# Other steps for the scores and transposes of three batches, for the sums of w2 and for the stores of two experts' w2

## The chip, the core and the metric

The kernel runs on one core of a Trainium2 chip. Its engines each run their own list of instructions in program order: PE (TensorE, the matmuls), DVE (VectorE), ACT (ScalarE), POOL (GpSimd) and SP (SyncE, which here only issues transfers). POOL and ACT issue transfers too. Between engines, work is ordered by semaphores. The metric is the time of one execution on the device in microseconds (us), as the median of the runs.

## The reference

The program is an attention over 32 memory slots followed by a mixture of four experts. All inputs are fp32.

```python
# q, k, v: (8, 8, 576, 64); phi: (8, 8, 576, 32)
a = softmax(phi, axis=seq)
k_m = einsum('bhsm,bhsd->bhmd', a, k)
v_m = einsum('bhsm,bhsd->bhmd', a, v)
attn = softmax(q @ k_m.T / sqrt(64), axis=-1) @ v_m
x = attn.transpose(0, 2, 1, 3).reshape(8 * 576, 512)
# experts: w1 (4, 512, 1024), w2 (4, 1024, 512), p = probs / sum(probs)
out = sum(p[:, e] * (relu(x @ w1[e]) @ w2[e]) for e in range(4))
```

## The kernel before

Every fp32 operand of a large product is kept as two parts, a rounded high part and the rest, and a product is three matmuls of the parts (high by high, high by rest, rest by high), added up in a PSUM bank. A split is a copy on ACT (the high part) and a subtraction on DVE or POOL (the rest).

The attention of a batch is never written out. `attn @ w1[e]` is computed as the softmax weights `AT` (32 slots of 8 heads by 576 rows) times `vw`, which is `v_m` times `w1[e]`. For experts 0 to 2 of the first four batches `vw` is made in place (L535 to L537). For expert 3 of these, and for the last four batches later on, one matmul pair makes it for four batches at once, the "four-batch products": L159 and L160 split the weight, L579 multiplies, L584 and L585 write the two parts into one of three buffers `vst`, POOL stores the buffer to memory (L567, `vwd`), and SP loads the pieces back as `vw` (L618).

**Steps.** The first four batches are worked off in two pairs of 128 steps each: 4 experts by 2 batches by 2 row halves by 8 column tiles of the hidden layer. Step s first adds up what the last group of eight has finished (`accumulate`, L696 on DVE), then runs what a table `plan` holds for s, then makes the hidden tile of step s + 2 (`first`: six matmuls L641 to L643, 256 or 320 wide, then the relu on ACT, L653, and its rest on DVE, L655) and the second product of step s (`second`: L674 to L676, 512 wide, six or nine matmuls). So a relu has two steps before its tile is used. From step 256 on come 64 units of four steps each, which do the last two pairs of batches with seven products of half-sized blocks instead of eight; these need sums of blocks of w2.

**What fills the plan.** `at(s, ...)` puts work into step s; nothing else decides the order.

- `attention(b, start, written, scores, turns)` does one batch's attention. Its numbers stand in the table `ATT`. phi is loaded at `start`, and k and v are multiplied from there on; `written` is where `v_m` is split. `scores` holds three steps n, for query tiles 0 and 1, 2 and 3, and 4: the score matmuls L463 at n, the maximum on DVE (L473, L476) at n + 1, the exponential on ACT (L483) at n + 2, the rest of the softmax on DVE (L490 to L493) at n + 3. `turns` holds three steps n: the transposes on PE (L514, which read L493's result `at`) at n, and the copies into `AT` (L525 on ACT, L526 on DVE) at n + 1, which give the bank back.
- `sums(s, home, lag, e, fh)` makes the sums for one half of an expert's w2; the table `JOBS` holds s, home and lag of each of the eight jobs, numbered from 0. At s SP loads two halves of a megabyte into the buffer `raw` (L201); there is one such buffer, so the load waits on SP until the last store of the job before has landed. At s + lag and s + lag + 1 DVE makes four sums (L225 to L228); at s + lag + 1 to s + lag + 4 ACT (L213) and POOL (L214) split them; at s + lag + 3 and s + lag + 5 POOL stores them (L219). In jobs of home "" the split parts live in buffers that a batch's phi and tail also use.
- `keep_w2(e, j)` stores the split w2 of the first pair in memory (L182, eight transfers of 0.5 MB per expert, by POOL for experts 1 to 3), to be loaded later. They are issued at steps 32 e + `KEEP_AT` + j.
- SP's loads of inputs go through four buffers `stage` (L145); taking one issues the load three further on in the order of use. The query tiles of the scores come this way, as `in_qm` and, for the last tile, `in_qt`.

Of the kernel before, what the change touches and what calls it, by code (L numbers as in the profile page):

```python
# [27 lines left out]
STEPS = 2 * 2 * NJ  # L28
PAIR = E * STEPS
# [21 lines left out]
PAIR_AT = ((18, 19, 26, 27), (28, 29, 30, 31))  # L51

ATT = {
    2: (22, 48, (92, 96, 100), (97, 101, 104)),
    3: (38, 65, (104, 107, 110), (112, 113, 114)),
    4: (PAIR, PAIR + 35, (PAIR + 34, PAIR + 37, PAIR + 41), (PAIR + 38, PAIR + 42, PAIR + 45)),
    5: (PAIR + 26, PAIR + 53, (PAIR + 76, PAIR + 80, PAIR + 84), (PAIR + 112, PAIR + 113, PAIR + 114)),
    6: (PAIR + 40, PAIR + 67, (2 * PAIR + 23, 2 * PAIR + 27, 2 * PAIR + 31), (2 * PAIR + 29, 2 * PAIR + 33, 2 * PAIR + 37)),
    7: (PAIR + 64, PAIR + 90, (2 * PAIR + 98, 2 * PAIR + 102, 2 * PAIR + 106), (2 * PAIR + 115, 2 * PAIR + 116, 2 * PAIR + 117)),
}  # L60

# [9 lines left out]
Q = 256  # L71
X_BANK, Y_BANK, AB_BANK = 4, 2, 6
JOBS = (
    (62, "", 4), (86, "", 4), (97, "", 4), (108, "", 4), (118, "", 4),
    (PAIR + 26, "AT", 4), (PAIR + 61, "a", 3), (PAIR + 87, "", 4),
)
KEEP_AT, W2_AGAIN = 20, 24
FOUR_AT_7 = ((0, 4, 8, 12), (16, 20, 24, 28))
VW_LOAD_7 = ((21, 37), (26, 41))
FIRST_LOADS = (PAIR + 112, PAIR + 121, PAIR + 122, PAIR + 123, PAIR + 124, PAIR + 125, PAIR + 126, PAIR + 127)  # L80
# [3 lines left out]
def body(ctx: ExitStack, tc: tile.TileContext, qm, qt, kv, kvt, phi, prob, w1, w1d, w2, out):  # L84
# [95 lines left out]
    def keep_w2(e, j):  # L180
        d = kept_for["w2", e, j] = dram.tile([P, 2, DM], F32, name=f"kw{e}{j}")
        (nc.gpsimd if e else nc.scalar).dma_start(d, w2t[0, e, j].bitcast(F32))  # L182
# [521 lines left out]
    def at(s, unit):  # L704
        plan[s].append(unit if isinstance(unit, tuple) else (None, unit))
# [112 lines left out]
        attention(b, *ATT[b])  # L818
    for e in range(E):
        for j in range(NJ):  # L820
            at(e * STEPS + KEEP_AT + j, lambda a=(e, j): keep_w2(*a))
    for n, job in enumerate(JOBS):
        sums(*job, n // 2, n % 2)
    for s in FIRST_LOADS:
# [19 lines left out]
    for block in range(UNITS // 4):  # L844
        e, fh = divmod(block % (2 * E), 2)
# [428 lines left out]
```

## Time and profile before

| | |
|---|---|
| median of 3 runs | 1399.04 us (1397.17 to 1401.68) |
| profiled execution | 1398.29 us, its span 1396.2 us |
| PE busy | 1365.6 us (98%) |
| DVE, ACT, POOL busy | 838.1, 625.5, 617.2 us (60%, 45%, 44%) |
| mean DMA traffic | 216 GB/s over the span |

A row of the timeline gives the start and the duration of an instruction in us, its engine, its line, what it writes and reads, and in brackets how long the engine stood before it and who ended that. Matmuls overlap: the time that one takes from PE is the distance from its start to the next one's, not its printed duration. `SPq` is the queue of transfers that SP issues. A row of the windows gives, for a stretch of time, the busy time of each engine with its number of instructions, then the granted TensorE clock as a share of the full one, the busy share of the DMA engines and what they moved.

### The profile page before, as it was taken

To read this page: it belongs to the slowest core of one execution; us is meant where nothing else is said; L and a number is where in the kernel's file an instruction comes from. 1 tells how busy PE (TensorE), PEld (TensorE's weight loads), DVE (VectorE), ACT (ScalarE), POOL (GpSimd) and SP (SyncE) were. 2 spreads that over 40 slices of the span, in tenths; PEclk is the share of its full clock that TensorE was granted. 3 is DMA by queue.
4 is the path that set the end of the run, shared out by engine and by line. 5 is a ranking of instruction groups with operands and counts; after the bars stand their busy time and mean duration, and the time that the engine had idled before them with its cause. 6 is when DMAs were issued, how large, how long until landed. Compare 5 with 4: busy or idle time off the path is not lost.

```text
span 1396.2 us, 25220 instructions
## 1 busy us (share of the span) xinstructions
PE 1365.6 (98%) x8894; PEld 1250.9 (90%) x8894; DVE 838.1 (60%) x1894; ACT 625.5 (45%) x1536; POOL 617.2 (44%) x652
## 2 busy tenths in 40 slices
PE   7999999999999999999999999999999999999998
PEld 6788888887878888889888998999999999999998
DVE  7875535446645365454434477767767666666666
ACT  6665555534335455554334344455443333333332
POOL 4400355755343415533145376677753344433333
PEclk9999999999999999999999999999999999999999
DMA  7742336798575354354599898999984776666662
GB/s 254 240 163 76 123 102 223 250 362 288 200 292 207 100 198 164 122 197 135 174 295 304 265 326 283 309 329 316 329 290 143 241 196 176 176 176 176 175 179 79
DMA packets 102029, 301.37 MB, mean 216 GB/s; under 512 B 24976, under 2 KB 26128, under 8 KB 101904
## 3 DMA queue, kind: packets, MB, share of 16 engines
q1 hardware_dynamic: 81168, 224.26, 51.8%
q0 software_dynamic: 19584, 71.31, 13.1%
q10 hardware_dynamic: 1152, 4.19, 0.8%
q8 instruction: 71, 1.16, 0.3%
q14 instruction: 54, 0.44, 0.1%
HBM read 213.46 MB, written 84.93 MB: 214 GB/s over the span
## 4 chain that ended last, share of the span: by engine, by line
PE 73%; DVE 3%; DMA 3%; POOL 2%; issue 1%; ACT 1%; SPq 0%; DVEq 0%; POOLq 0%; ACTq 0%
PE banks L1002 22%; PE banks L674 6%; PE banks L675 6%; PE banks L676 6%; PE banks L916 5%; PE banks L917 5%; PE banks L918 5%; PE banks L641 3%; PE banks L642 3%; PE banks L643 3%; PE banks L579 2%; PE banks L463 2%; PE banks L357 1%; PE banks L1040 1%; PE banks L1041 1%
## 5 line engine op out<-in xcount | busy, mean ns | idle before, releaser
L1020 DVE SCALAR_TENSOR_TENSOR acc<-banks,pt,acc 128x256 f32<-128x256 f32 x416 | 200.0, 481 | 108.9 <-PE banks L1002 105.2
L160 POOL TENSOR_TENSOR w<-stage,w 128x512 fp32r<-128x512 f32 x134 | 176.6, 1319 | 191.2 <-ACT w L159 180.9
L655 DVE SCALAR_TENSOR_TENSOR h<-banks,h 128x256 fp32r<-128x256 f32 x256 | 107.5, 421 | 174.1 <-ACT h L653 106.6
L674 PE MATMUL banks<-w,h 128*128 128x512 f32 x512 | 203.0, 396 | 1.4 <-DVE acc L696 1.3
L676 PE MATMUL banks<-w,h 128*128 128x512 f32 x512 | 201.9, 394 | 1.9 <-DVE h L655 1.9
L675 PE MATMUL banks<-w,h 128*128 128x512 f32 x512 | 202.3, 395 | 0.0
L653 ACT ACTIVATE h<-banks 128x256 fp32r<-128x256 f32 x256 | 97.9, 384 | 206.8 <-PE banks L643 163.8
L641 PE MATMUL banks<-AT,vw 128*128 128x256 f32 (+1 forms) x512 | 156.7, 306 | 3.9 <-DVE vw L556 2.1
L1002 PE MATMUL banks<-w,a 128*128 128x256 f32 x1080 | 154.7, 282 | 0.3 <-DVE acc L1020 0.2
L643 PE MATMUL banks<-AT,vw 128*128 128x256 f32 (+1 forms) x512 | 151.0, 296 | 1.2 <-DVE vw L556 1.2
L916 PE MATMUL banks<-AT,vw 128*128 128x256 f32 (+1 forms) x512 | 151.8, 296 | 0.0
L642 PE MATMUL banks<-AT,vw 128*128 128x256 f32 (+1 forms) x512 | 151.5, 296 | 0.2 <-DVE AT L526 0.2
L917 PE MATMUL banks<-AT,vw 128*128 128x256 f32 (+1 forms) x512 | 151.3, 295 | 0.0
L918 PE MATMUL banks<-AT,vw 128*128 128x256 f32 (+1 forms) x512 | 151.0, 295 | 0.0
L1002 PEld LDWEIGHTS banks<-w,a 128*128 128x128 f32 x1080 | 143.6, 189 | 4.8 <-issue 0.9
L983 POOL TENSOR_TENSOR vt<-ph,vt 128x512 fp32r<-128x512 f32 x64 | 84.1, 1314 | 107.8 <-ACT vt L982 78.2
L346 POOL TENSOR_TENSOR kvs<-stage,kvs 128x512 fp32r<-128x512 f32 x58 | 75.2, 1316 | 104.8 <-ACT kvs L345 98.7
L676 PEld LDWEIGHTS banks<-w,h 128*128 128x128 f32 x512 | 96.8, 189 | 24.0 <-DVE h L655 2.3
L641 PEld LDWEIGHTS banks<-AT,vw 128*128 128x128 f32 x512 | 96.7, 189 | 14.6 <-DVE vw L556 4.8
L674 PEld LDWEIGHTS banks<-w,h 128*128 128x128 f32 x512 | 96.8, 189 | 13.7 <-DVE acc L696 1.7
L675 PEld LDWEIGHTS banks<-w,h 128*128 128x128 f32 x512 | 96.9, 189 | 10.9
L159 ACT CAST w<-stage 128x512 fp32r<-128x512 f32 x168 | 102.8, 619 | 4.6 <-DMA stage<-in_w 2.3
(149 smaller groups left out, 2982.5 us busy)
## 6 DMA issues: line engine op xcount, KB each, us to landing
w<-kw SPq DMA_DIRECT2D x93, 512.0 KB, 5.5
vwd<-vst POOLq DMA_DIRECT2D x80, 512.0 KB, 6.2
vw<-vwd SPq DMA_DIRECT2D x320, 128.0 KB, 5.7
w<-v SPq DMA_DIRECT2D x55, 512.0 KB, 5.7
stage<-in_w SPq DMA_DIRECT2D x44, 512.0 KB, 4.4
stage<-in_w1d SPq DMA_DIRECT2D x40, 512.0 KB, 4.9
stage<-in_kv SPq DMA_DIRECT2D x32, 512.0 KB, 4.1
kw<-w POOLq DMA_DIRECT2D x24, 512.0 KB, 7.1
```

Source lines behind the costliest of these rows:

```text
L160: eng.tensor_sub(dst[:, 1, :], raw, dst[:, 0, :].bitcast(F32))
L641: nc.tensor.matmul(ps, w[:, 0, f], at_t[:, g, 0, c], start=g == 0, stop=False)
L642: nc.tensor.matmul(ps, w[:, 0, f], at_t[:, g, 1, c], start=False, stop=False)
L643: nc.tensor.matmul(ps, w[:, 1, f], at_t[:, g, 0, c], start=False, stop=g == 1)
L674: nc.tensor.matmul(po[t], x[:, 0, :], w[:, 0, :], start=j == 0, stop=False)
L675: nc.tensor.matmul(po[t], x[:, 0, :], w[:, 1, :], start=False, stop=False)
L676: nc.tensor.matmul(po[t], x[:, 1, :], w[:, 0, :], start=False, stop=j == NJ - 1)
L916: nc.tensor.matmul(ps, w[:, 0, f], at_t[:, g, 0, c], start=g == 0, stop=False)
L917: nc.tensor.matmul(ps, w[:, 0, f], at_t[:, g, 1, c], start=False, stop=False)
L918: nc.tensor.matmul(ps, w[:, 1, f], at_t[:, g, 0, c], start=False, stop=g == 1)
L1002: nc.tensor.matmul(ps, a[:, l, jj], w[:, r, c], start=start and jj + i == 0, stop=jj == 1 and i == 2, skip_group_check=True,)
L1020: VE.scalar_tensor_tensor(a, src, p, a, ALU.mult, ALU.add)
```

## The change

Only tables change, and `KEEP_AT` becomes a tuple with a value per expert. No instruction is added or removed.

```diff
--- before.py
+++ after.py
@@ -51,11 +51,11 @@
 PAIR_AT = ((18, 19, 26, 27), (28, 29, 30, 31))
 
 ATT = {
-    2: (22, 48, (92, 96, 100), (97, 101, 104)),
-    3: (38, 65, (104, 107, 110), (112, 113, 114)),
-    4: (PAIR, PAIR + 35, (PAIR + 34, PAIR + 37, PAIR + 41), (PAIR + 38, PAIR + 42, PAIR + 45)),
+    2: (22, 48, (91, 95, 101), (97, 102, 106)),
+    3: (38, 65, (105, 108, 111), (113, 115, 117)),
+    4: (PAIR + 2, PAIR + 37, (PAIR + 34, PAIR + 37, PAIR + 41), (PAIR + 38, PAIR + 42, PAIR + 45)),
     5: (PAIR + 26, PAIR + 53, (PAIR + 76, PAIR + 80, PAIR + 84), (PAIR + 112, PAIR + 113, PAIR + 114)),
-    6: (PAIR + 40, PAIR + 67, (2 * PAIR + 23, 2 * PAIR + 27, 2 * PAIR + 31), (2 * PAIR + 29, 2 * PAIR + 33, 2 * PAIR + 37)),
+    6: (PAIR + 40, PAIR + 67, (2 * PAIR + 23, 2 * PAIR + 27, 2 * PAIR + 35), (2 * PAIR + 31, 2 * PAIR + 33, 2 * PAIR + 39)),
     7: (PAIR + 64, PAIR + 90, (2 * PAIR + 98, 2 * PAIR + 102, 2 * PAIR + 106), (2 * PAIR + 115, 2 * PAIR + 116, 2 * PAIR + 117)),
 }
 
@@ -71,10 +71,10 @@
 Q = 256
 X_BANK, Y_BANK, AB_BANK = 4, 2, 6
 JOBS = (
-    (62, "", 4), (86, "", 4), (97, "", 4), (108, "", 4), (118, "", 4),
-    (PAIR + 26, "AT", 4), (PAIR + 61, "a", 3), (PAIR + 87, "", 4),
+    (62, "", 5), (86, "", 5), (97, "", 5), (108, "", 5), (119, "", 5),
+    (PAIR + 26, "AT", 4), (PAIR + 61, "a", 4), (PAIR + 87, "", 5),
 )
-KEEP_AT, W2_AGAIN = 20, 24
+KEEP_AT, W2_AGAIN = (20, 12, -1, 20), 24
 FOUR_AT_7 = ((0, 4, 8, 12), (16, 20, 24, 28))
 VW_LOAD_7 = ((21, 37), (26, 41))
 FIRST_LOADS = (PAIR + 112, PAIR + 121, PAIR + 122, PAIR + 123, PAIR + 124, PAIR + 125, PAIR + 126, PAIR + 127)
@@ -818,7 +818,7 @@
         attention(b, *ATT[b])
     for e in range(E):
         for j in range(NJ):
-            at(e * STEPS + KEEP_AT + j, lambda a=(e, j): keep_w2(*a))
+            at(e * STEPS + KEEP_AT[e] + j, lambda a=(e, j): keep_w2(*a))
     for n, job in enumerate(JOBS):
         sums(*job, n // 2, n % 2)
     for s in FIRST_LOADS:
```

Batch 2's scores move from steps 92, 96, 100 to 91, 95, 101 and its last transposes from 104 to 106; batch 3's scores come at 105, 108, 111 instead of 104, 107, 110 and its transposes at 113, 115, 117 instead of 112, 113, 114. Batch 4 starts two steps later. Batch 6's third scores go from step 287 to 291, its transposes from 285, 289 and 293 to 287, 289 and 295. Six jobs of `sums` get lag 5 instead of 4 and one lag 4 instead of 3; job 4 also loads a step later. Expert 1's stores go from steps 52 to 59 to 44 to 51, expert 2's from 84 to 91 to 63 to 70. Three places of the new order:

On POOL at the end of the first four-batch products, before: `kw` are the keep stores of expert 2, `vwd` the stores of the products, L160 the splits of their weights.

```order
L567 DMA vwd_3052<-vst 128x1024
L160 TENSOR_TENSOR w_3061<-stage,w_3061 128x512
L182 DMA kw_3064<-w_2400 128x1024
L567 DMA vwd_3086<-vst 128x1024
L160 TENSOR_TENSOR w_3093<-stage,w_3093 128x512
L182 DMA kw_3096<-w_2427 128x1024
L567 DMA vwd_3118<-vst 128x1024
L182 DMA kw_3125<-w_2461 128x1024
L567 DMA vwd_3148<-vst 128x1024
L182 DMA kw_3155<-w_2498 128x1024
L567 DMA vwd_3178<-vst 128x1024
```

And now, on POOL ahead of the first product store (L214 and L219 are the splits and stores of job 0's sums):

```order
L160 TENSOR_TENSOR w_2609<-stage,w_2609 128x512
L182 DMA kw_2612<-w_2549 128x1024
L214 TENSOR_TENSOR raw<-raw,sv 128x512
L182 DMA kw_2634<-w_2571 128x1024
L214 TENSOR_TENSOR raw<-raw,sv 128x512
L160 TENSOR_TENSOR w_2655<-stage,w_2655 128x512
L182 DMA kw_2658<-w_2609 128x1024
L219 DMA v_2660<-sv 256x1x512
L219 DMA v_2660<-raw 256x1x512
L214 TENSOR_TENSOR raw<-raw,sv 128x512
```

The eight keep stores of expert 2 no longer stand between the last product stores; the last of them stand among the splits of the sums, ahead of every product store.

On SP around batch 2's last query tile, `in_qt`, before; the `vw` rows are the last two of eight loads of one batch and half, the raw load that of job 2:

```order
L618 DMA vw<-vwd_3148 32x1024
L618 DMA vw<-vwd_3178 32x1024
L145 DMA stage<-in_qt 128x256
L145 DMA stage<-in_qm 128x1024
L201 DMA raw<-in_w 128x1024 x2
```

and now:

```order
L618 DMA vw<-vwd_2934 32x1024
L145 DMA stage<-in_w 128x1024 x2
L145 DMA stage<-in_qt 128x256
L618 DMA vw<-vwd_2966 32x1024
L618 DMA vw<-vwd_2996 32x1024
```

The load of `in_qt` stands ahead of the eight `vw` loads that it followed (the first two of them are shown); the raw load still follows them.

On DVE around batch 2's last softmax (the rows of 64 partitions), before, with the sums of job 2 (L225 to L228) and the relus' rests (L655):

```order
L655 SCALAR_TENSOR_TENSOR h<-banks,h 128x256
L526 TENSOR_TENSOR AT<-banks,AT 128x2x256
L227 TENSOR_TENSOR raw<-raw 128x2x256
L228 TENSOR_TENSOR raw<-raw 128x2x256
L655 SCALAR_TENSOR_TENSOR h<-banks,h 128x256
L655 SCALAR_TENSOR_TENSOR hm<-banks,hm 128x64
L490 TENSOR_REDUCE z<-at 64x8
L491 TENSOR_SCALAR z<-z 64x8
L492 RECIPROCAL z<-z 64x8
L493 TENSOR_TENSOR at<-at,z 64x256
L655 SCALAR_TENSOR_TENSOR h<-banks,h 128x256
L655 SCALAR_TENSOR_TENSOR hm<-banks,hm 128x64
```

and now:

```order
L526 TENSOR_TENSOR AT<-banks,AT 128x2x256
L227 TENSOR_TENSOR raw<-raw 128x2x256
L228 TENSOR_TENSOR raw<-raw 128x2x256
L655 SCALAR_TENSOR_TENSOR h<-banks,h 128x256
L655 SCALAR_TENSOR_TENSOR hm<-banks,hm 128x64
L696 SCALAR_TENSOR_TENSOR acc<-banks,pt,acc 128x512 x2
L490 TENSOR_REDUCE z<-at 64x8
L491 TENSOR_SCALAR z<-z 64x8
L492 RECIPROCAL z<-z 64x8
L493 TENSOR_TENSOR at<-at,z 64x256
L655 SCALAR_TENSOR_TENSOR h<-banks,h 128x256
L655 SCALAR_TENSOR_TENSOR hm<-banks,hm 128x64
```

The accumulation L696 now stands ahead of this softmax, not behind it, and more relus stand between the softmax and what follows.

## The prediction

> **What bounds the kernel now.** I read the page's busy shares first, then the matrix engine's timeline for every place where a matmul's start stands further from the one before than its kind usually does, then who ended each such wait, and last the windows for the traffic around it.
>
> ```profile
> PE 1365.6 (98%) x8894; PEld 1250.9 (90%) x8894; DVE 838.1 (60%) x1894; ACT 625.5 (45%) x1536; POOL 617.2 (44%) x652
> 307.65 0.50 PE L674 MATMUL banks<-w,h 128*128 128x512 f32 x1 [1.28 <-DVE acc L696]
> 337.37 0.68 PE L463 MATMUL banks<-kT,stage 128*64 128x64 f32 x8 [1.32 <-DMA stage<-in_qt]
> 349.48 0.33 PE L514 MATMUL banks<-ident,at 64*128 64x64 f32 x2 [2.08 <-DVE at L493]
> 412.89 0.50 PE L535 MATMUL banks<-w,vt 128*128 128x512 f32 x1 [1.45 <-DVE h L655]
> 414.20 0.39 PE L641 MATMUL banks<-AT,vw 128*128 128x256 f32 x1 [0.34 <-DVE vw L556]
> 522.32 0.39 PE L641 MATMUL banks<-AT,vw 128*128 128x256 f32 x1 [1.82 <-DVE h L655]
> 872.32 0.68 PE L463 MATMUL banks<-kT,stage 128*64 128x64 f32 x8 [1.66 <-DVE AT L526]
> ```
>
> PE is busy for 98% of the span, so the time is its matmuls plus its few stalls. The change removes no matmul: all it can win is in the stalls. The rows are the large ones after the head of the program. Five places belong to batches 2, 3 and 6, to w2 sums or to expert 2's stores, which the change moves; the wait of 1.82 us at 522.32 belongs to batch 5 and job 5, whose steps do not move, so it stays.
>
> Two stalls cost more than their idle time, because the granted clock falls to half after them.
>
> ```profile
> core 0: us, PE busy (x) PEld busy (x) DVE busy (x) ACT busy (x) POOL busy (x), PEclk, DMA share, GB/s
> 350.10:356.90 6.80, 6.80 (x27) 6.32 (x27) 2.53 (x7) 1.17 (x4) 2.43 (x3) 0.50 0.94 326
> 415.00:418.40 3.40, 3.40 (x10) 2.72 (x9) 2.19 (x4) 3.33 (x7) 1.88 (x2) 0.50 1.00 395
> ...
> 307.99 0.40 PE L675 MATMUL banks<-w,h 128*128 128x512 f32 x1
> 308.22 0.39 PE L676 MATMUL banks<-w,h 128*128 128x512 f32 x1
> 325.21 2.00 PE L463 MATMUL banks<-kT,stage 128*128 128x64 f32 x16
> 349.74 3.37 PE L463 MATMUL banks<-kT,stage 128*128 128x64 f32 x16
> 352.87 0.61 PE L641 MATMUL banks<-AT,vw 128*128 128x320 f32 x1
> 357.06 0.31 PE L641 MATMUL banks<-AT,vw 128*128 128x320 f32 x1
> 357.21 0.31 PE L642 MATMUL banks<-AT,vw 128*128 128x320 f32 x1
> 415.09 0.63 PE L674 MATMUL banks<-w,h 128*128 128x512 f32 x1
> 418.67 0.39 PE L641 MATMUL banks<-AT,vw 128*128 128x256 f32 x1
> ```
>
> At full clock a score group of 16 takes 2.00 us, a 512-wide matmul 0.23 us, a 320-wide one 0.15 us, start to start. After the wait at 349.48 the score group takes 3.37 us (1.37 lost), and the next six 320-wide and six 512-wide take 357.06 - 352.87 = 4.19 us instead of 6 x 0.15 + 6 x 0.23 = 2.28 (1.91 lost). After the wait at 412.89 nine 512-wide take 418.67 - 415.09 = 3.58 us instead of 2.07 (1.51 lost).
>
> **The change part by part.** The causes stand on the other engines.
>
> ```profile
> 295.62 0.53 POOL L567 DMA_DIRECT2D vwd<-vst  x1
> 305.29 0.59 ACT L584 CAST vst<-banks 128x512 fp32r<-128x512 f32 x1 [5.23 <-DMA vwd<-vst]
> 331.89 0.39 SPq L145 DMA_DIRECT2D stage<-in_qt  x1
> 327.31 0.68 POOL L219 DMA_DIRECT2D v<-raw  x1 [0.47 <-PE banks L463]
> 336.94 0.80 SPq L201 DMA_DIRECT2D raw<-in_w  x2
> 342.82 0.69 DVE L225 TENSOR_TENSOR raw<-raw 128x512 f32<-128x512 f32 x1 [2.23 <-DMA raw<-in_w]
> 411.08 0.69 DVE L225 TENSOR_TENSOR raw<-raw 128x512 f32<-128x512 f32 x1 [5.69 <-DMA raw<-in_w]
> 870.00 1.67 DVE L493 TENSOR_TENSOR at<-at,z 128x512 f32<-128x512 f32 x1
> ```
>
> *A, 307.65.* A product's store, issued at 295.62 between expert 2's keep stores on the same queue, released its buffer to ACT 9.67 us later; ACT stood for 5.23 us with the relus behind it, DVE behind ACT, PE behind DVE's accumulation. With the eight stores gone from there this falls: -1.3 us (-1.55 with the slow first matmul; I take -1.5).
>
> *B, 337.37.* The query load of batch 2's last tile was issued at 331.89, behind eight loads of vw. Now it stands ahead of them on SP, and its scores come a step later. SP reaches it some 6 us sooner, and 1.32 us were missing: -1.4 us.
>
> *C, 349.48.* Job 2's raw load waits on SP for the last store of job 1, issued at 327.31; it goes out at 336.94, DVE gets it at 342.82 and had waited 2.23 us; sums, a softmax and with it the transpose ran late. Now store, load, sums and softmax come one step later and the transpose two. That wins a step of slack, about 2.8 us (6 x 0.23 + 6 x 0.15, and a score group's or copy's share), less two accumulations that now stand ahead of the softmax (1.4 us), against 2.1 us of lateness. If job 1's store still takes 9.6 us, some 0.8 us of waiting is left; if it takes what such stores take otherwise, nothing is. I take all of it, 2.08 + 1.37 + 1.91: -5.4 us; -4.6 as the poor bound, since waits of 1.28 to 1.82 us left the clock alone.
>
> *D, 412.89.* DVE stood 5.69 us for job 4's raw, and PE idled 1.45 + 0.34 us, so that some 3.9 us of DVE's wait were hidden. Job 3's store and with it the load come a step later, the sums two: a step (about 2.8 us) is won, and a wait of 2.9 us is under the 3.9. The price of the whole is 1.79 + 1.51 and some 0.4 of restarts, 3.7; with four chances in five: -3.0 us.
>
> *E, 872.32.* The third score group of batch 6 needed the bank that DVE frees behind a softmax whose last operation took 1.67 us. The transposes now come a step after, these scores four steps later: -1.6 us.
>
> Sum won: 1.5 + 1.4 + 5.4 + 3.0 + 1.6 = 12.9 us.
>
> *F, what the keep stores meet in their new place.* POOL issues eight more transfers in steps 63 to 70, just ahead of the four-batch products.
>
> ```profile
> L182 POOL DMA_DIRECT2D kw<-w x24: 531/554/832, 203.1 to 410.7; - x24
> 237.87 1.29 POOL L160 TENSOR_TENSOR w<-stage,w 128x512 fp32r<-128x512 f32 x1 [1.57 <-ACT w L159]
> 247.10 1.30 POOL L214 TENSOR_TENSOR raw<-raw,sv 128x512 fp32r<-128x512 f32 x1 [1.41 <-ACT sv L213]
> 259.47 1.02 POOL L567 DMA_DIRECT2D vwd<-vst  x1
> 258.36 0.59 ACT L584 CAST vst<-banks 128x512 fp32r<-128x512 f32 x1 [1.22 <-PE banks L579]
> 261.09 0.59 ACT L584 CAST vst<-banks 128x512 fp32r<-128x512 f32 x1 [1.22 <-PE banks L579]
> 266.90 0.59 ACT L584 CAST vst<-banks 128x512 fp32r<-128x512 f32 x1 [4.31 <-DMA vwd<-vst]
> 269.42 0.50 PE L579 MATMUL banks<-w,vs 128*128 128x512 f32 x1 [0.43 <-POOL w L160]
> 240.00:260.00 20.00, 20.00 (x112) 17.61 (x111) 12.58 (x24) 10.44 (x26) 18.18 (x17) 1.00 0.54 154
> 300.00:320.00 20.00, 18.72 (x110) 16.20 (x109) 9.54 (x18) 5.27 (x14) 7.80 (x12) 1.00 1.03 401
> ```
>
> An issue takes POOL 0.55 us, 4.4 us for eight; six fall into gaps like those of 1.57 and 1.41 us. From 247.10 to 259.47 POOL has no gap. That stretch now begins a step later (2.1 us), without one split that goes ahead of it (1.3) and with two issues in it (1.1): the first product store goes out some 1.9 us later, near 261.4. The first three stores have buffers of their own; the fourth cast waits for the first. At 266.90 it had waited 4.31 us, which cost PE 0.43. With the same 7.4 us from issue to release it would be 1.9 us later and cost PE up to as much; with the page's median of 6.2 us for such stores, 0.7. The bytes allow it: eight halves of a megabyte, 4.2 MB in 20 us, add 210 to the 154 GB/s of 240 to 260, under the 401 of 300 to 320. I take +1.0 us, bounds 0 and +2.5.
>
> *G, the rest.* Expert 1's keep stores go into steps 44 to 51, where POOL has gaps of the same kind; batch 4's chain starts two steps later and meets the splits of the next w1; the transposes of batch 6 take the two banks in another order. None of it stands in the trace. Below, 0; above, one wait like the 1.3 us of A or B in one of the three places. +0.5 us, being nearest to places where waits of 0.3 to 0.5 us stand now.
>
> Sum: 12.9 - 1.0 - 0.5 = 11.4 us. The profiled execution took 1398.3 us (span 1396.2 and 2.1 around it), so 1386.9; the median of the runs is 0.7 above it: **1387.6 us**.
>
> **The rivals.** *1: late data come back.* The raw loads still hang on the stores of the job before, a chain that the lag moves along with it; if C keeps a wait above 2 us and D keeps its own, 8.4 of the 12.9 us stay away: 1396.0; with D alone, 1390.6. For it speaks that stores and loads are delayed together; against it that 4.2 MB leave the very stretch in which the store took 9.6 us. Taken together, about 1393.
>
> *2: the halved clock has another cause than the idle time.* Then the 1.37 + 1.91 + 1.51 = 4.8 us stay and it comes out at 1392.4. Against it: both falls follow the longest waits of their stretch; for it: the 1.82 us at 522.32 and 1.66 at 872.32 were followed by none. [...]
>
> *3: given away again.* The stalls wander to the next place where DVE and POOL run in order (steps 124 to 133, where batch 4's first tile waits for job 4's stores): 12.9 us are eaten, 1398. Against it: DVE is busy for 60% only.
>
> *4: slower.* The keep stores stretch every product store to the 9.67 us seen at 295.62. A buffer then turns in 1.1 us (cast at 258.36 to issue at 259.47) plus 9.67, a tile each 3.6 us over three buffers, against 2.73 us a step (258.36 to 261.09): 16 tiles lose 0.86 us each, 13.8, plus the 2.5 of F's bound and 1.3 of G: 17.6 - 12.9 = 4.7, so 1403. It decides from 3 x 2.73 - 1.1 = 7.1 us per store on; the first one already takes 7.4. Against it: in the new order all keep stores of expert 2 stand ahead of the first product store, and none follows.
>
> **How the numbers follow.** The forecast (1383 to 1391) has 0.56, rival 1 0.19, rival 2 0.05, rival 3 0.12, rival 4 0.08. A measurement tells this kernel from no change from about 0.3% on, 4.2 us: faster means under 1394.8. Most of rival 1 and all of rival 2 are there: faster 0.78; same 0.14; slower 0.08. The range runs from 1382 to 1398. Below: D whole (0.7), nothing for F and G (1.5), the 1.8 us at 522.32 dissolved by the shifted timing, and the spread of the runs (1.9 from their median to the lowest) make 1381.7. Above: rivals 1 and 3.
>
> **What would show it.** A right: no ACT wait of 5 us for a product store before step 90. B right: the query load's issue ahead of the vw loads, no wait at its scores. C and D right: a granted clock of 1.0 from 340 to 420. E right: no wait for AT at batch 6's scores. F: the wait of ACT near 267 within 2 us of the 4.31. The prediction is wrong if ACT waits for product stores all through steps 76 to 88, if a raw load still ends a PE stall above 2 us, or if the clock falls to half at a new place.

## The result and the profile after

| | before | after |
|---|---|---|
| median, six runs each | 1400.0 us | 1392.1 us (1389.8 to 1396.2) |
| ratio | | 0.9949, interval 0.9932 to 0.9966 |
| profiled execution's span | 1396.2 us | 1390.3 us |
| median, the change run again later (12 runs beside 23 of before) | 1399.3 us | 1394.5 us, ratio 0.9969, interval 0.9956 to 0.9982 |

The kernel became faster, by 7.1 us by the first ratio and 4.3 by the second; neither interval contains 1. The forecast was 11.4 us. The traces of the two kernels differ by 5.9 us of span, and that can be laid out by stages. A stage here is the distance between the starts of the first L641 of two steps, so it holds the work and the waits of PE in it; the last one ends with PE's last matmul. The letters are those of the prediction:

| steps | what lies there | before | after | after, second run |
|---|---|---|---|---|
| 72 to 84 | four-batch products (F) | 36.5 | 40.8 | 38.5 |
| 84 to 92 | their end (A) | 24.5 | 23.1 | 23.1 |
| 92 to 112 | batches 2 and 3, job 2 (B, C) | 59.4 | 54.2 | 55.6 |
| 112 to 130 | job 4 (D) | 54.7 | 51.9 | 51.9 |
| 130 to 200 | batch 4 and 5, jobs 5 and 6 | 203.6 | 203.0 | 204.5 |
| 200 to PE's last matmul | the units, batch 6 (E) | 758.1 | 758.0 | 758.1 |

So 1.4 + 5.2 + 2.8 + 0.6 + 0.1 = 10.1 us were won and 4.3 lost in the first of the two traces. First PE's rows of the profile after, with the timeline's large waits in the places the prediction spoke of:

```profile
PE 1362.0 (98%) x8894; PEld 1248.4 (90%) x8894; DVE 841.3 (61%) x1894; ACT 625.4 (45%) x1536; POOL 617.4 (44%) x652
271.65 0.47 PE L579 MATMUL banks<-w,vs 128*128 128x512 f32 x1 [2.53 <-ACT h L653]
272.71 0.79 PE L579 MATMUL banks<-w,vs 128*128 128x512 f32 x1 [0.59 <-POOL w L160]
341.63 0.50 PE L676 MATMUL banks<-w,h 128*128 128x512 f32 x1 [2.03 <-DVE h L655]
342.75 0.68 PE L463 MATMUL banks<-kT,stage 128*64 128x64 f32 x8
516.45 0.39 PE L641 MATMUL banks<-AT,vw 128*128 128x256 f32 x1 [1.83 <-DVE h L655]
866.27 0.98 PE L1002 MATMUL banks<-w,tl 128*128 128x256 f32 x6 [1.22 <-DVE acc L1020]
```

The waits near 308, 337, 349 and 413 are gone; the scores at 342.75 no longer wait for `in_qt`. Three stand where none, or a smaller one, stood: 2.53 + 0.59 us at 271 (0.43 before), 2.03 at 341, 1.22 at 866. The next rows are the windows after, with the columns of the prediction's windows:

```profile
272.40:275.80 3.40, 3.09 (x10) 2.80 (x11) 1.87 (x5) 2.29 (x7) 3.36 (x5) 0.50 0.64 123
340.00:360.00 20.00, 18.37 (x109) 15.88 (x110) 13.17 (x32) 6.37 (x19) 7.83 (x8) 1.00 0.66 230
400.00:420.00 20.00, 19.47 (x106) 16.54 (x106) 12.36 (x21) 10.93 (x22) 6.80 (x8) 1.00 1.02 381
```

The clock is whole from 340 to 360 and from 400 to 420. It is at half for 3.4 us behind the wait at 271 instead, a new place. In the second trace of the same kernel the waits near 270 are 0.40 and 0.58 us and the clock stays whole there, but it is at half behind the relu wait, which is 2.04 us long at 339.14:

```profile
339.00:342.40 3.40, 3.26 (x13) 2.30 (x14) 0.75 (x3) 0.00 (x0) 0.00 (x0) 0.50 0.57 148
```

That is why steps 92 to 112 took 55.6 us there instead of 54.2: of the traces below with this wait of 2.0 us, the six with such a fall behind it have 55.6 or 55.7 there, the two without have 54.2. The causes of the three new waits in the first trace, on the engines behind them:

```profile
261.16 1.10 POOL L567 DMA_DIRECT2D vwd<-vst  x1
270.19 0.58 ACT L584 CAST vst<-banks 128x512 fp32r<-128x512 f32 x1 [7.52 <-DMA vwd<-vst]
...
334.10 5.49 POOL L160 TENSOR_TENSOR w<-stage,w 128x512 fp32r<-128x512 f32 x4
334.44 5.19 DVE L491 TENSOR_SCALAR z<-z 128x16 f32<-128x16 f32 x1
346.94 0.69 DVE L225 TENSOR_TENSOR raw<-raw 128x512 f32<-128x512 f32 x1 [0.95 <-DMA raw<-in_w]
...
864.00 1.27 POOL L160 TENSOR_TENSOR w<-stage,w 128x512 fp32r<-128x512 f32 x1 [1.43 <-ACT w L159]
864.17 1.66 DVE L493 TENSOR_TENSOR at<-at,z 128x512 f32<-128x512 f32 x1
865.75 0.47 DVE L1020 SCALAR_TENSOR_TENSOR acc<-banks,pt,acc 128x256 f32<-128x256 f32 x1
```

ACT waits 7.52 us for the first product store, issued 9.03 us earlier. DVE's L491, an addition on 128 x 16 numbers with a median of 0.18 us, takes 5.19 us and ends at 339.63, with the last of four POOL splits that run without a pause until 339.59; the relus behind it come late. And batch 6's softmax still ends in a multiplication of 1.66 us (its median is 0.69), which starts 0.17 us after a POOL split does, with an accumulation now waited for behind it instead of a copy.

### The profile page after: what moved, and what is told of

Same layout as the page of the kernel before. It is cut to its first block, busy times and chain, and to the rows that moved or that the text cites. A ratio compares the mean times of both kernels' runs of the same rounds, so it can differ in the third digit from the quotient of the medians.

```text
span 1390.3 us, 25223 instructions
## 1 busy us (share of the span) xinstructions
PE 1362.0 (98%) x8894; PEld 1248.4 (90%) x8894; DVE 841.3 (61%) x1894; ACT 625.4 (45%) x1536; POOL 617.4 (44%) x652
## 3 DMA queue, kind: packets, MB, share of 16 engines
q1 hardware_dynamic: 81168, 224.26, 51.9%
## 4 chain that ended last, share of the span: by engine, by line
PE 89%; DVE 4%; DMA 2%; issue 2%; ACT 1%; SPq 0%; POOL 0%; DVEq 0%; ACTq 0%; POOLq 0%
PE banks L1002 22%; PE banks L676 9%; PE banks L674 9%; PE banks L675 9%; PE banks L916 5%; PE banks L917 5%; PE banks L918 5%; PE banks L641 5%; PE banks L642 4%; PE banks L643 4%; PE banks L579 3%; PE banks L463 2%; PE banks L357 2%; DMA stage<-in_w 1%; PE banks L1040 1%
## 5 line engine op out<-in xcount | busy, mean ns | idle before, releaser
L160 POOL TENSOR_TENSOR w<-stage,w 128x512 fp32r<-128x512 f32 x134 | 177.0, 1332 | 188.7 <-ACT w L159 179.4
L655 DVE SCALAR_TENSOR_TENSOR h<-banks,h 128x256 fp32r<-128x256 f32 x256 | 107.3, 420 | 168.6 <-ACT h L653 111.4
L641 PE MATMUL banks<-AT,vw 128*128 128x256 f32 (+1 forms) x512 | 156.6, 306 | 3.7 <-DVE h L655 1.8
L641 PEld LDWEIGHTS banks<-AT,vw 128*128 128x128 f32 x512 | 96.8, 189 | 13.8 <-DVE vw L556 3.8
```

Source lines behind the costliest of these rows:

```text
L160: eng.tensor_sub(dst[:, 1, :], raw, dst[:, 0, :].bitcast(F32))
L641: nc.tensor.matmul(ps, w[:, 0, f], at_t[:, g, 0, c], start=g == 0, stop=False)
```

## The experiments

Each was timed beside the kernel before. In the three sessions (four rows of the table each) before stood at 1398.8, 1397.7 and 1399.3 us; ratios are to the runs of the same session.

| run | median, us | ratio, interval |
|---|---|---|
| expert 2's stores back | 1391.9 | 0.9963, 0.9950 to 0.9976 |
| keep stores alone, on the kernel before | 1398.1 | 0.9996, 0.9985 to 1.0007 |
| expert 2's stores by ACT | 1393.0 | 0.9964, 0.9951 to 0.9976 |
| old lags | 1393.2 | 0.9968, 0.9957 to 0.9980 |
| without L491 | 1389.7 | 0.9944, 0.9930 to 0.9958 |
| half of the stores late | 1390.2 | 0.9941, 0.9929 to 0.9953 |
| batch 6 back | 1393.8 | 0.9977, 0.9962 to 0.9992 |
| without L491, all stores late | 1387.7 | 0.9924, 0.9912 to 0.9936 |
| the change again | 1394.5 | 0.9969, 0.9956 to 0.9982 |
| batch 6 back again | 1396.0 | 0.9973, 0.9961 to 0.9986 |
| job 1 at lag 4, half of the stores late | 1389.1 | 0.9931, 0.9915 to 0.9947 |
| job 1 at lag 4, all stores late | 1390.9 | 0.9946, 0.9930 to 0.9961 |

The intervals are 3 to 4.5 us wide, as wide as most of the effects; what decides is the stage in the trace.

### What delays the first product store

Two things stand in front of it that did not before: eight keep stores, and job 0's last stores, a step later by the lag. The first run takes away the stores, the fourth the lag; the second puts the keep stores of the change (expert 1's and expert 2's) into the kernel before.

```diff
-KEEP_AT, W2_AGAIN = (20, 12, -1, 20), 24
+KEEP_AT, W2_AGAIN = (20, 12, 20, 20), 24
```

> The changed kernel with only expert 2's keep stores put back to steps 84 to 91 (table entry -1 back to 20). In the changed kernel ACT waits 7.5 us at 270.19 for the first product store and PE loses 5.0 us there, against 0.7 before. Theory K (the eight early keep stores do it): the wait at 267 to 270 falls back to about 4.3 us, PE loses 0.7 there, and ACT's wait of about 5 us for a product store before step 90 returns with 1.5 us of PE; in all 2.8 us less than the changed kernel, about 1389.3. Rival L (job 0's lag of 5 does it, because its last stores now go out right ahead of the first product store): the wait stays at about 7 us, the stall near 308 returns on top, about 1393.6.

The second, on the kernel before:

```diff
-KEEP_AT, W2_AGAIN = 20, 24
+KEEP_AT, W2_AGAIN = (20, 12, -1, 20), 24
...
-            at(e * STEPS + KEEP_AT + j, lambda a=(e, j): keep_w2(*a))
+            at(e * STEPS + KEEP_AT[e] + j, lambda a=(e, j): keep_w2(*a))
```

> The kernel before with only the new steps of the keep stores (experts 1 and 2). Theory K: the wait near 267 grows to 7 us and costs PE 4 us more, the 1.5 us near 308 go, the 2.2 us of DVE's wait for raw near 343 fall because the store before it meets less traffic: slower than before by 0 to 3 us, 1400 to 1403. Rival L: the wait near 267 stays near 4.3 us, and only gains are left: 1396 to 1398.5.

The fourth, on the change:

```diff
-    (62, "", 5), (86, "", 5), (97, "", 5), (108, "", 5), (119, "", 5),
-    (PAIR + 26, "AT", 4), (PAIR + 61, "a", 4), (PAIR + 87, "", 5),
+    (62, "", 4), (86, "", 4), (97, "", 4), (108, "", 4), (118, "", 4),
+    (PAIR + 26, "AT", 4), (PAIR + 61, "a", 3), (PAIR + 87, "", 4),
```

> The changed kernel with the old table of jobs (lags 4 and 3, job 4 loading at 118). Theory K: the wait near 270 stays above 6 us, since the keep stores stay early; rival L: it falls to 4.3 us and PE's loss there from 5.0 to 0.7. In either case DVE waits for raw again (2 to 3 us near 343, 5 us near 410), and PE idles for it by 1.5 to 2 us near 412 with the clock at half after it, so 3 to 4 us come back: by K about 1395.5, by L about 1391.5.

ACT's row for the first buffer that has to come back, with the keep stores put back, and with the old lags:

```profile
266.79 0.58 ACT L584 CAST vst<-banks 128x512 fp32r<-128x512 f32 x1 [3.30 <-DMA vwd<-vst]
```

```profile
270.60 0.58 ACT L584 CAST vst<-banks 128x512 fp32r<-128x512 f32 x1 [5.99 <-DMA vwd<-vst]
```

With the keep stores back the wait is 3.30 us and steps 72 to 84 take 36.2 us, as before the change; steps 84 to 92 take 24.6 again. With the old lags and the early stores it is 5.99 us and 39.7. In the kernel before with the keep stores alone, steps 72 to 84 take 38.7 and 84 to 92 take 23.0. Theory K holds: in all fourteen traces of this document steps 72 to 84 take 38.0 us or more where eight stores go out early, and 36.9 or less where at most four do. The lag of job 0 has no part in it that the rows show, though with the old lags and the early stores (the second and the fourth run) steps 6 to 72 take 195.6 to 195.8 us instead of 194.5, with a PE wait of 0.85 us near 256.

The second run shows one thing more. Nothing but stores moved in it, and yet steps 92 to 112 take 54.8 us instead of 59.4, a new wait of 1.75 us for L493 at 332.29 included. PE's rows at the scores of the last query tile and at the transpose that waited 1.32 and 2.08 us before:

```profile
339.15 0.68 PE L463 MATMUL banks<-kT,stage 128*64 128x64 f32 x8
349.60 0.34 PE L514 MATMUL banks<-ident,at 64*128 64x64 f32 x2 [0.39 <-DVE at L493]
```

So the stores alone take away the stalls that the forecast called B and C, clock included. The first run, with expert 2's stores in their old place and the new tables, takes them away too (54.2 us). Either part of the change suffices there, and their gains do not add. The second run's time is still 0.9996 of before, since its trace pays in other places: 2.2 us in steps 72 to 84, 1.5 in steps 6 to 72, and twice 1.6 us for a halved clock behind the waits of batches 5 and 6, which in before's trace are there with the clock whole. No run moves expert 1's stores by themselves.

The expected 1389.3 us of the first run did not come (1391.9). Its profiled execution shows two things that ate the gain, in steps that the edit does not move: after the wait for batch 5's relu the clock was at half for 3.4 us (steps 130 to 200 took 204.5 instead of 203.0), and the head of the program up to step 6 was 1.1 us longer.

Whether it is POOL's time or the bytes was asked by issuing the same stores from ACT:

```diff
-        (nc.gpsimd if e else nc.scalar).dma_start(d, w2t[0, e, j].bitcast(F32))
+        (nc.scalar if e in (0, 2) else nc.gpsimd).dma_start(d, w2t[0, e, j].bitcast(F32))
```

> The changed kernel with expert 2's eight keep stores issued by ACT instead of POOL in the same steps: the same bytes at the same time, but no time of POOL (4.4 us less) and not in POOL's queue. If POOL's issue time is what delays the first product store, it goes out about 1.7 us sooner (259.5 instead of 261.2), ACT's wait near 270 falls from 7.5 to about 4.5 us and the kernel gains 3 to 4 us: 1388 to 1389. If the bytes on the DMA engines do it, the wait stays near 7 us and the time within 1 us of 1392.

The rows of ACT in this run, and then the windows of 250 to 260 and 260 to 270 of before, of the change, and of the run with the keep stores back:

```profile
269.55 0.58 ACT L584 CAST vst<-banks 128x512 fp32r<-128x512 f32 x1 [6.86 <-DMA vwd<-vst]
```

```profile
250.00:260.00 10.00, 10.00 (x54) 8.79 (x53) 4.63 (x12) 5.25 (x15) 10.00 (x11) 1.00 0.65 192
260.00:270.00 10.00, 9.57 (x49) 8.04 (x48) 3.37 (x9) 4.04 (x11) 5.89 (x8) 1.00 0.94 350
```

```profile
250.00:260.00 10.00, 10.00 (x53) 8.69 (x52) 4.66 (x12) 5.86 (x16) 9.98 (x11) 1.00 0.88 301
260.00:270.00 10.00, 9.11 (x45) 7.26 (x44) 1.78 (x5) 1.50 (x4) 5.87 (x8) 1.00 0.98 358
```

```profile
250.00:260.00 10.00, 10.00 (x55) 8.80 (x54) 4.40 (x12) 5.90 (x16) 10.00 (x10) 1.00 0.59 177
260.00:270.00 10.00, 10.00 (x52) 8.63 (x51) 3.69 (x9) 3.88 (x12) 7.27 (x9) 1.00 0.99 361
```

With no time of POOL spent on them the first product store is issued at 261.33, no earlier than in the change (261.16), the wait is 6.86 us and the stage 42.2 us: POOL's issue time is not the cause. The first store is also issued at nearly the same time in the change (261.16) and with the keep stores back (260.77), yet it takes 9.03 us to the release in the one and 6.02 in the other. From 260 to 270 the share of the DMA engines is 0.94, 0.98 and 0.99 in these three, and 1.00 in the run with the stores from ACT. What differs is the ten microseconds ahead, 0.59 and 0.65 against 0.88; over all fourteen traces that share is 0.81 to 0.97 with the eight stores early and 0.55 to 0.68 with none or four of them there. The reading is that the other transfers due at that time are slowed, and reach into the stretch from 260 on. This carry-over is inferred from the shares; no run measured a single transfer's path.

Half of the bytes, on the change:

```diff
-            at(e * STEPS + KEEP_AT[e] + j, lambda a=(e, j): keep_w2(*a))
+            at(e * STEPS + KEEP_AT[e] + j + 21 * (e == 2 and j > 3), lambda a=(e, j): keep_w2(*a))
```

> The changed kernel with expert 2's keep stores in two halves: parts 0 to 3 in steps 63 to 66 as now, parts 4 to 7 in steps 88 to 91, behind the last product store. If the bytes ahead of the first product store are what delays it, half of them give back at least half of the stretch: ACT's wait near 270 falls from 7.5 us to 4 to 5.5 us, PE loses 0.7 to 2 us there instead of 5.0, no wait of 5 us for a product store comes before step 90: 1388 to 1389.5. If only the first issue counts or the four others disturb the sums of job 1, about 1392.

Steps 72 to 84 take 36.9 us, 0.4 more than before the change, and 84 to 92 take 23.1, as in the change. The time is 1390.2 us, above the expected 1388 to 1389.5, since steps 92 to 112 took 55.6 us, with the clock at half for 3.4 us behind the relu wait of 2.03 us at 338.27.

### What holds DVE in the softmax

```diff
-        nc.vector.tensor_scalar_add(zv[:, :, 0], zv[:, :, 0], 1e-9)
```

> The changed kernel without the addition of 1e-9 to the softmax sums of the slots' weights (L491; left out of the computation: the sums are at least 1, so the addition changes no fp32 value). In the changed kernel this operation on 128 x 16 values took 5.19 us at 334.44 and ended with POOL's last split of a row without pause, at 339.59; DVE's relus then came late and PE idled 2.2 us at 341. Theory P (this form of operation cannot start while POOL works, the ones beside it can): with it gone the reciprocal goes through at its 0.25 us, the idle time at 341 disappears and the kernel gains 2 to 2.6 us, 1389.5 to 1390. Rival Q (any DVE operation on these buffers would stand there until POOL pauses): the reciprocal or the multiplication waits instead, about 4 us, and the time stays within 0.6 us of 1392.

The median, 1389.7 us, is what theory P asked for (though its ratio, 0.9944, is not told apart from the change's 0.9949), and P is wrong all the same. The rows of POOL, DVE and PE in this run (its lines are one lower from there on: L491 is the reciprocal, L492 the multiplication):

```profile
331.77 5.49 POOL L160 TENSOR_TENSOR w<-stage,w 128x512 fp32r<-128x512 f32 x4
331.63 0.25 DVE L491 RECIPROCAL z<-z 128x16 f32<-128x16 f32 x1
331.92 5.90 DVE L492 TENSOR_TENSOR at<-at,z 128x512 f32<-128x512 f32 x1
338.80 0.50 PE L675 MATMUL banks<-w,h 128*128 128x512 f32 x1 [2.01 <-DVE h L654]
```

The reciprocal passes in 0.25 us, the multiplication behind it takes 5.90 us instead of 0.69 and ends half a microsecond after POOL's four splits (331.77 + 5.49 = 337.26), and PE waits its 2.01 us as in the change. So it is not this addition alone. Beside POOL's splits the addition of a constant took 5.19 us in the change (median 0.18) and the product of two tiles 5.90 us here (median 0.69), while in the change a reduction took its usual 0.68 us at 324.04, during two splits, and a reciprocal its usual 0.25 us at 325.65, during the split from 325.53 to 326.81. Why the one pair and not the other, no run shows.

How long the addition takes beside splits differs. The first softmax of the change, on DVE and POOL:

```profile
324.75 0.86 DVE L491 TENSOR_SCALAR z<-z 128x16 f32<-128x16 f32 x1
324.28 1.30 POOL L214 TENSOR_TENSOR raw<-raw,sv 128x512 fp32r<-128x512 f32 x1
325.53 1.28 POOL L160 TENSOR_TENSOR w<-stage,w 128x512 fp32r<-128x512 f32 x1
```

Here the addition was over with the split at hand, although the next one followed without a pause; at 334.44 it stood through the rest of a row. What decides between the two, no run shows.

The time of the run without L491 was won elsewhere. Against the first trace of the change it took 2.7 us less in steps 72 to 84 (ACT's wait was 4.88 us; the same order gives 38.0 to 41.3 us there from run to run), 1.1 less ahead of step 72 and 1.8 less behind step 200, and 2.5 more in steps 84 to 112, with the clock at half behind the wait of 2.01 us. Behind step 200 PE's wait of 1.22 us is gone, and batch 6's softmax shows why:

```profile
862.22 0.69 DVE L492 TENSOR_TENSOR at<-at,z 128x512 f32<-128x512 f32 x1
862.27 1.79 POOL L160 TENSOR_TENSOR w<-stage,w 128x512 fp32r<-128x512 f32 x1 [1.43 <-DVE z L491]
```

In the change the multiplication starts 0.17 us behind this split and takes 1.66 us, the split 1.27. Without the addition it starts 0.05 us ahead and takes 0.69, the split 1.79, and PE stands for neither. So the slow multiplication behind E's wait goes with the same meeting of DVE and POOL, and in these two traces the one that started second was the longer one: DVE by 0.97 us in the change, POOL by 0.52 here.

The row's end and the softmax's start are both set by tables. With job 1 at its old lag its splits lie a step earlier:

```diff
-    (62, "", 5), (86, "", 5), (97, "", 5), (108, "", 5), (119, "", 5),
+    (62, "", 5), (86, "", 4), (97, "", 5), (108, "", 5), (119, "", 5),
...
-            at(e * STEPS + KEEP_AT[e] + j, lambda a=(e, j): keep_w2(*a))
+            at(e * STEPS + KEEP_AT[e] + j + 21 * (e == 2 and j > 3), lambda a=(e, j): keep_w2(*a))
```

> The changed kernel with job 1 at lag 4 again (its splits on POOL a step earlier) and expert 2's keep stores in two halves, steps 63 to 66 and 88 to 91. If POOL's unbroken row of work is what holds the second softmax's operation on DVE (5.19 us), it now meets the first softmax instead, as with the old lags, whose result is wanted three steps later, and PE no longer idles near 340: 2.5 to 4 us less than the changed kernel there, and 2 to 3 us less near 270: 1386 to 1388. If the lag of 5 was needed for raw, DVE waits over 4 us for it near 345 and PE idles there: 1389 to 1391.

DVE's two softmaxes in this run:

```profile
321.62 5.12 DVE L491 TENSOR_SCALAR z<-z 128x16 f32<-128x16 f32 x1
333.08 0.83 DVE L491 TENSOR_SCALAR z<-z 128x16 f32<-128x16 f32 x1
342.04 0.69 DVE L225 TENSOR_TENSOR raw<-raw 128x512 f32<-128x512 f32 x1 [0.63 <-DMA raw<-in_w]
```

Now the first softmax has the long addition, 5.12 us, and PE does not wait for it at all: steps 92 to 112 take 51.9 us, 2.3 to 3.8 under the change and as little as with the old lags (51.9 there too, with DVE's wait for raw at 2.18 us). The median is 1389.1, 5.4 us under the change in the same session; 1386 to 1388 were expected, and of the rest 1.6 us are a clock fallen behind batch 5's wait and 1.6 the stall near 308, which stands here again. No keep store lies between the product stores in this run; ACT waits all the same:

```profile
305.82 0.59 ACT L584 CAST vst<-banks 128x512 fp32r<-128x512 f32 x1 [4.07 <-DMA vwd<-vst]
```

In the change ACT's largest wait there is 3.18 us and PE does not stand; at 4.07 it does. Both traces with keep stores among the product stores (before, and expert 2's stores back) show that stall; without them it is near, and in the run without L491 0.80 us of it stood behind an ACT wait of 4.75.

The same with all eight stores late:

```diff
-KEEP_AT, W2_AGAIN = (20, 12, -1, 20), 24
+KEEP_AT, W2_AGAIN = (20, 12, 24, 20), 24
...
-    (62, "", 5), (86, "", 5), (97, "", 5), (108, "", 5), (119, "", 5),
+    (62, "", 5), (86, "", 4), (97, "", 5), (108, "", 5), (119, "", 5),
```

> The same with expert 2's keep stores in steps 88 to 95. No product store is disturbed: PE loses under 1 us near 270 and 308. DVE's wait for raw near 345 was 4.75 us with these steps and lag 5; a step earlier for job 1's stores leaves some 2 to 3 us, which the relus' two steps hide: 1385 to 1387. If it does not fall, PE idles near 350 by 1 to 2 us: 1388.

The time missed: 1390.9 us. The rows of POOL, DVE and PE:

```profile
330.45 6.35 POOL L160 TENSOR_TENSOR w<-stage,w 128x512 fp32r<-128x512 f32 x5
331.49 5.35 DVE L491 TENSOR_SCALAR z<-z 128x16 f32<-128x16 f32 x1
338.84 0.50 PE L676 MATMUL banks<-w,h 128*128 128x512 f32 x1 [3.20 <-DVE h L655]
```

The products went undisturbed (35.6 us for steps 72 to 84, the least of all), but POOL's splits were pushed together into five in a row, at the second softmax again, and steps 92 to 112 took 57.3 us. DVE's wait for raw, on which the expectation turned, was zero. With the same lag the stage took 51.9 us where the row fell on the first softmax and 57.3 where it fell on the second: here the place of the row mattered, not the lag.

Both edits with the addition left out:

```diff
-KEEP_AT, W2_AGAIN = (20, 12, -1, 20), 24
+KEEP_AT, W2_AGAIN = (20, 12, 24, 20), 24
...
-        nc.vector.tensor_scalar_add(zv[:, :, 0], zv[:, :, 0], 1e-9)
```

> The changed kernel without the addition of 1e-9 and with expert 2's eight keep stores in steps 88 to 95, all behind the last product store. Theory: neither place of the product stores is disturbed (PE loses 0.7 us near 270 and nothing near 308), and the softmax does not wait for POOL: 2.5 + 4.3 us under the changed kernel, about 1385.5. Rival: the stores now meet those of job 1 and the vw loads between 315 and 340, raw of job 2 comes late again, and 2 to 5 us come back there: 1388 to 1391.

It had the lowest median and the lowest ratio of all, 1387.7 us, though not the expected 1385.5. Here the first softmax's multiplication was the long one (3.88 us at 321.37), the second took 0.80, and raw came 4.75 us late at 344.76, at some 0.7 us of PE. It leaves the addition out, and part of its gain is that: behind step 200, where none of these stores lies, it takes 1.3 us less than the change.

### Whether batch 6's new steps are worth anything

```diff
-    6: (PAIR + 40, PAIR + 67, (2 * PAIR + 23, 2 * PAIR + 27, 2 * PAIR + 35), (2 * PAIR + 31, 2 * PAIR + 33, 2 * PAIR + 39)),
+    6: (PAIR + 40, PAIR + 67, (2 * PAIR + 23, 2 * PAIR + 27, 2 * PAIR + 31), (2 * PAIR + 29, 2 * PAIR + 33, 2 * PAIR + 37)),
```

> The changed kernel with batch 6's scores and transposes at their old steps. The changed kernel's trace has 0.34 + 1.38 + 0.44 us of waits there (862, 866, 877), the one before 1.82 + 0.41 (872, 883). If the term was worth its 1.6 us, this run is that much slower, 1393.7; if the wait has only moved to the accumulations behind the same softmax, which is what the trace says, the time stays within 0.4 us of 1392 and the wait of 1.7 us for AT is back near 866.

It stood at 1393.8 us in a session without the change, so it was run once more beside it:

> The changed kernel itself once more, on the chip and beside the runs that the next three are compared with. Its order near 270 is that of three earlier runs, in which ACT waited 5.5 to 7.5 us for the first product store and PE lost 1.6 to 5.5 us; if this cost varies from run to run with the same order, ACT's wait is again between 5 and 8 us but PE's loss not again 5.0; the median lies between 1390.5 and 1393.5.

> Batch 6's steps put back, once more, beside the changed kernel. If the wait there has only moved, as the trace says, the two medians differ by under 1.5 us; if the term was worth its 1.6 us or more, this one is 1.6 to 4 us above the changed kernel.

Beside each other: 1394.5 for the change and 1396.0 with batch 6 back, ratios 0.9969 and 0.9973 with intervals of 0.0026: not told apart. The traces say more. From step 200 to PE's last matmul the change took 758.0 and 758.1 us; with the old steps it took 758.1 in the kernel before and in one run, and 759.7 in two others. The windows behind the wait for `AT` in one run of 759.7 (the 0.61 is a mean: the clock was at half from 871.1 to the end of the window), and in the run of 758.1:

```profile
870.30:874.00 3.70, 3.70 (x23) 3.63 (x22) 2.50 (x6) 1.14 (x3) 0.90 (x2) 0.61 0.97 352
```

```profile
865.30:869.00 3.70, 3.70 (x32) 3.55 (x31) 3.11 (x8) 1.22 (x3) 1.02 (x3) 1.00 0.84 308
```

The wait itself only moved, as the trace after had said. What the new steps take away is the chance that the clock is halved behind the old wait of 1.7 us, which costs 1.6 us where it happens. With two of four traces, and none of the ten with the new steps, that is a likely reading, not a shown one.

The change run again also answered for F: with the same order, ACT waited 5.39 us and steps 72 to 84 took 38.5 us, where the first trace had 7.52 and 40.8. The two runs with batch 6 back, of the same order there, took 38.0 and 41.3. In the two short ones the clock stayed whole, in the two long ones it was at half for 3.4 us.

## Why the prediction was right or wrong

**The direction and the range held; the gain was well over what came, and the agreement is in part luck.** 1387.6 us was forecast, 1392.1 and 1394.5 were measured, inside 1382 to 1398 but outside the band of 1383 to 1391 that had the largest chance. The gain was to be 11.4 us and was 7.1 and 4.3. Of A to E's 12.9 us the first trace has 9.5 (1.4, 5.2, 2.8 and 0.1) and the second 8.0; against them stand, where 1.5 us were forecast for F and G, 3.7 us (4.3 lost in F, 0.6 won in batch 4's and 5's steps) and 3.0 us (2.0 and 0.9 lost, the latter to the clock). By one of its own signs the forecast was wrong: the clock fell to half at a new place, at 272.4 in the first trace and at 339.0 in the second. Its sign for F, ACT's wait within 2 us of 4.31, failed in the first (7.52) and held in the second (5.39), and these waits also break A's sign, no ACT wait of 5 us before step 90.

**A held.** Steps 84 to 92 won 1.4 us against 1.5 forecast, and with the keep stores back the stall is back (24.6 us).

**B and C: the waits went, but the cause was not shown to be the one named, and the price was short.** The wait at the query tile and that at the transpose are gone, and the raw load comes with 0.95 us of waiting or none. The forecast gave B to the order on SP and C to a step of slack for job 2. The keep stores alone, with neither, take both away (54.8 us); so do the new tables with expert 2's stores back (54.2). And B and C were to win 6.8 us together, and won 5.2 and 3.8. The step that failed is "a step of slack is won": the slack was counted against late data, and what the later splits do to DVE was put at nothing. The splits of job 1 came a step later on POOL, and the second softmax stood in their way: before, its L491 took 0.82 us, now it met POOL where that works without a pause, and took 5.19. The row of 3.04 us for the same operation, ending with a POOL split, stood in the timeline of before (at 323.20). With job 1 a step earlier the same stage gives 7.5 us, more than was forecast.

**D held**: 2.8 us against 3.0, and no halved clock. With the old lags the stage is back at 54.6 us, so the lag won it.

**E failed.** The wait was put down to the bank and to where the transposes stand; what PE waited for came behind DVE's softmax with its slow multiplication (1.67 us before, 1.66 after), which started 0.16 and 0.17 us behind the start of a POOL split. The change moved the transposes, not that. Whoever is next behind it on DVE is then late: now an accumulation. 0.1 us of 1.6 came. Where the multiplication came first, in the run without L491, it took 0.69 us and the stage 1.8 us less.

**F was mis-sized, and its upper bound too.** 1.0 us, at most 2.5, was forecast; 4.3 came in the first trace, with the clock at half for 3.4 us in it, and 2.0 in the second without. The delay of the first store's issue was right (1.7 us later, 1.9 forecast). Wrong was that "the bytes allow it": 364 GB/s on the mean of twenty microseconds lies under 401, but the share of the engines was 0.88 from 250 to 260 and 0.98 from 260 to 270, and, by the reading above, what is late by then is not made up before the products need their buffers. By its own formula, a store above 7.1 us costs; it took 9.03. That formula is not the whole of it: in the second trace the store took 6.9 us, and the stage still lost 2.0.

**G**: a small gain, 0.6 us (a PE wait of 0.37 us at 477, in batch 4's stage, is gone) instead of a loss of 0.5.

**The rivals.** Rival 1 had nearly the right time, 1393, by the wrong mechanism: data do not come late, DVE does. Rival 4's mechanism is F's, for the first store and not for all sixteen, so it cost 2 to 4.3 us instead of 17.6. Rival 2 is out, since between the head of the program and PE's last matmul every fall of the clock stands at a wait of PE; but what spoke for it holds too, as not every such wait is followed by one. Rival 3 did not happen at steps 124 to 133 (0.5 us of waiting at 419); its 1398 does not follow from its terms either, 1387.6 + 12.9 being 1400.5.

## What to carry to other kernels

Before work is moved along one engine's order, list for its neighbours not only who waits for whom by a semaphore but which of their operations take longer than their median there: in the kernel before, in the change and with job 1 at lag 4 an addition on DVE with a median of 0.18 us took 3.0 to 5.4 us and ended within 0.1 us of a POOL split, and no row named POOL. Eight stores moved ahead of a stretch with a DMA share of 0.94 to 0.99 went with 4.3 us lost there in the first trace of the change and 2.0 in the second, though by the mean of twenty microseconds there was room (an estimated 364 under 401 GB/s); look at the ten microseconds ahead and at who needs the first transfer after it. Where two parts of a change serve the same stall, try each by itself before adding their gains. And where effects are smaller than the spread of the medians, compare stages of the traces; the time alone would have confirmed a theory here that the trace refuted.

## What the runs showed of the hardware

**An operation on DVE ended with POOL's row of splits.** L491 (median 0.18 us), or the multiplication in its place (median 0.69), took 3.0 us before, 5.2 in the change, 5.9 without the addition, 5.1 and 5.4 with job 1 at lag 4; in these traces L491 ended within 0.1 us of the end of a POOL split, and in the change it lasted through four of them, from 334.44 to 339.63. It did not always take so long (0.86 us at 324.75), and in one place POOL was the longer one: its split took 1.79 us instead of 1.27 where DVE's multiplication had begun 0.05 us earlier (862.22, without the addition).

**The clock behind a wait differed from run to run.** The wait for batch 5's relu is the same in all kernels (1.82 to 1.84 us). The rows of it, and of the 4 us behind it, in the change and in the run with expert 2's stores back:

```profile
516.45 0.39 PE L641 MATMUL banks<-AT,vw 128*128 128x256 f32 x1 [1.83 <-DVE h L655]
516.60:520.50 3.90, 3.90 (x25) 3.46 (x26) 2.81 (x6) 3.02 (x8) 3.90 (x5) 1.00 0.66 259
```

```profile
514.26 0.38 PE L641 MATMUL banks<-AT,vw 128*128 128x256 f32 x1 [1.84 <-DVE h L655]
514.40:518.50 4.10, 4.10 (x17) 3.45 (x18) 2.74 (x5) 2.54 (x6) 4.10 (x5) 0.61 0.63 245
```

Behind 1.83 us the clock stayed whole in one; behind 1.84 it was at half in the other, for 3.4 us from 515.3 on, at 1.6 us in the stage of steps 130 to 200. Of the fourteen traces, six show it and eight do not. Of the eight with a relu wait of 2.0 to 2.1 us near 340, six show it, at 1.5 us in steps 92 to 112. Between the head of the program and PE's last matmul every fall lasted 3.4 us, or 6.8 in two places. Behind a relu wait of 1.8 to 2.1 us the stage was thus longer by another 1.5 or 1.6 us in twelve of these 22 cases; the runs of one kernel spread by more than that (1389.8 to 1396.2 for the change).
